# Scores and state products by head in 64x32 tiles, and a reordered first block, in a state-attention and two-FFN kernel

## The chip, the cores and the metric

The kernel runs on one core of a Trainium2 chip. A core has TensorE (PE in the profile; its weight loads are PEld), VectorE (DVE), ScalarE (ACT), GpSimd (POOL) and SyncE (SP), which here issues nearly all DMAs. SBUF is the working memory, PSUM holds eight banks of 128 partitions by 512 fp32 numbers into which TensorE writes. The metric is device time in microseconds (us), the median of three runs.

## The reference

```python
def _attn_ref(x, state):                     # x: 8 batches, 8 heads, 512 tokens, 64; state: 32 states
    scale = 1.0 / np.sqrt(D)
    scores = scale * np.matmul(x, state.transpose(0, 1, 3, 2))
    a = softmax(scores)                      # over the 32 states
    xread = np.matmul(a, state)
    scores2 = scale * np.matmul(state, x.transpose(0, 1, 3, 2))
    a2 = softmax(scores2)                    # over the 512 tokens
    sread = np.matmul(a2, x)
    return np.concatenate([xread, sread], axis=2)

x = attn_out as (8 * 544, 512)               # heads side by side
h = x @ w_in;  g = np.maximum(0.01 * h, h);  x = g @ w_out        # 512 -> 2048 -> 512
g = x @ w_gate;  out = (silu(g) * (x @ w_val)) @ w_out2           # 512 -> 1536 -> 512
```

The weights arrive as 64-bit floats; the kernel makes fp32 of them itself.

## The kernel before

**Layer 1 folds the reading of the states into w_in.** For tokens, `x_read @ w_in` equals `a @ (state @ w_in)`. So the kernel computes, for each batch b, each group g of 512 columns of w_in (four groups) and each head, a product of the 32 states with the 64 rows of w_in that belong to the head. Four heads make one half q (two pairs of heads p = 2q and 2q+1; a pair lies on 128 partitions, its two heads e on 64 each), so a tile `sw` of 128 rows (4 heads x 32 states) by 512 columns stands for (b, g, q). It is split into a high and a low part (`swh`, `swl`), and the attention `a` into `ah` and `al`; every product of large matrices is done as three passes (`passes`, L437): low times high, high times low, high times high.

**The products come in two ways.** Batch 0's are made in place: `state_win` (L452) multiplies `states`, a tile in which a pair's two heads stand block-diagonally (128 rows by 64 columns, zeros elsewhere, filled by ScalarE copies from the loaded tile `flat` in `place_states`), with a chunk of w_in; two such matmuls fill one PSUM bank, `keep_sw_h` (ScalarE) and `keep_sw_l` (VectorE) split it from the bank. All the others go through DRAM: `product_sw` (L461) multiplies, for one g and one pair, the states of four batches (bs = 0 or 1) of one head, 64 rows by 128 columns, with the head's half of the chunk; both heads go into two banks, ScalarE copies these to staging tiles, and `store_sw` writes them to `sw_dram` (for bs = 0 without batch 0's rows). There are 4 x 4 x 2 = 32 such products. Later `load_sw` fetches the 128 rows of one (b, g, q), and `split_sw_h` and `split_sw_l` split them.

**Scores.** `read_state` (L309) makes, for one b and q, the scores of 512 tokens: two matmuls of `states` (128 x 64) with the transposed tokens `xt` into one bank, a copy out (`scores_out`), the softmax over states on VectorE and ScalarE, and the split into `ah` and `al`. `read_tokens` (L374) makes the other softmax later: `turn` (four transposes, bank a), `read` (32-column products, bank b) and `read_out`.

**Slots.** Layer 1 runs in 8 x 16 slots, one for each batch j and each 128 of the 2048 hidden columns f. A slot has `h_mm` (six matmuls for the slot after next), `h_act` (leaky ReLU on ScalarE, high part on ScalarE, low part on VectorE) and `y_mm` (twelve matmuls into the four banks of `ps_y`). Other work is put into slots by `put` (L1306): it gives each step a start slot, waits for the step before, and moves a step on while VectorE's load in a slot (its "cost") would exceed a budget. A step's part W (ScalarE) runs at the head of the slot, D (VectorE) next, A after the first part of `h_act`, P (TensorE) and L (ScalarE) at the end. `sw_steps` load and split the products of later batches, `keep_steps` make batch 0's for g = 1 to 3 in the slots of `KEEP`.

**Opening and first block.** Everything is issued in program order, each engine taking its own instructions in that order. Before slot 0 the letters of `START` give the order, in slots 0 to 15 those of `SLOT0`: `c` advances by one of four steps the conversion of a weight chunk of 64-bit floats (two ScalarE operations, four VectorE operations: `limit`, `sign`, `join`, `add`; for chunks of w_out also a split into high and low), `p` makes one product that is ready, `0` and `1` the next step of batch 0's scores and softmax for q = 0 and 1, `h` a kept product of g = 0, `l` its low part, `m` and `M` the first hidden blocks; `H`, `S`, `L` are h_mm and the rest of h_act, `Y` and `Z` y_mm's halves, `D` and `A` the parts of the steps. `ORDER` is the order of the 32 chunks of w_in (`i`) and w_out (`o`), `LOADS` that of the first loads. A chunk of w_in is also stored to `win_dram`, for the 256 tail tokens at the end of layer 1. From slot 16 on the weights of layer 2 are converted in the background (`fill`).

PSUM banks: two for `ps_h`, four for `ps_y`, and banks a and b of `ps_a` for all else. Layer 2 (from about 690 us) is not touched.

Of the kernel before, what the change touches and what calls it, by code (L numbers as in the profile page):

```python
# [25 lines left out]
def kernel(  # L26
# [65 lines left out]
    SLOT0 = [  # L92
        "DcHcpAccccSYLpcZccc",
        "DcHcAcccpSYLpccZccc",
        "DcHcpccAcSYLpZccp",
        "cDccHcApSccYLpcZcccc",
        "cDcHccApScYLcZpc",
        "cccDHpccAccScYLpccZ",
        "ccDcHAcpScccYcLpZc",
        "ccDccHcApSccYcLpcZ",  # L100
        "cDcHcpcASYLpcccZ",
        "ccDHcAScYcpLccZcp",
        "ccDcHcASYcpLccZcp",
        "cDHccApSccYLccZ",
        "pcDHccASccYLcpcZ",
        "cpcDcHAccSYLccpccZp",
        "DcpcHcccpAcSYLcpZ",
        "pDpcHccpAcSYLcZp",
    ]
    KEEP = (0, 1, 3, 5, 8, 7)  # L110
# [39 lines left out]
    states = first1.tile([P, NPAIR, B, 2 * NS], F32, name="states")  # L150
# [10 lines left out]
    sw_dram = [[dram.tile([H, P, 512], F32, name=f"sw_dram{bs}_{g}") for g in range(FB)] for bs in range(B // 4)]  # L161
# [12 lines left out]
    def next_xt(n):  # L174
        for _ in range(min(n, len(pairs_t))):
            b, p = pairs_t.pop(0)
            xt[b, p] = xin.tile([P, S], F32, tag="xt", name="xt")
            nc.sync.dma_start(out=xt[b, p], in_=x_t[b, p])
# [54 lines left out]
    def convert(keys, room, prepare, load_next, finish=None):  # L233
# [4 lines left out]
        while todo or before or (finish and done):  # L238
# [15 lines left out]
            if key:  # L254
                ops["low"]()
                ops["sign"]()
# [52 lines left out]
    def read_state(b, q, bank):  # L309

        pairs = (2 * q, 2 * q + 1)
        v = {}

        def scores():

            ps = v["ps"] = ps_a.tile([P, 512], F32, tag=bank, name="ps_s")
            for i, p in enumerate(pairs):
                nc.tensor.matmul(  # L318
                    ps[2 * NS * i:2 * NS * (i + 1)], lhsT=states[:, p, b, :], rhs=xt.pop((b, p)),
                    start=True, stop=True,  # L320
                )
            next_xt(2)

        def scores_out():
            v["s"] = S_[b, q] = at1.tile([P, S], F32, tag="s", name="s", bufs=4)
            nc.scalar.copy(v["s"], v["ps"])


        def softmax_max():
            v["st"] = at1.tile([P, S], F32, tag="st", name="st", bufs=2)  # L330
            v["m1"] = at1.tile([P, S // NS], F32, tag="m1", name="m1", bufs=2)
            nc.vector.transpose(out=v["st"], in_=v["s"])
# [30 lines left out]
        def split_a_l():  # L363
# [3 lines left out]
            {"P": [scores], "L": [scores_out]},  # L367
# [6 lines left out]
    def read_tokens(b, q):  # L374
# [32 lines left out]
        def read():  # L407
# [3 lines left out]
            for i in range(2):  # L411
                for c in range(NC):
                    for k in range(4):
                        n = c * P + NS * (2 * i + k // 2)
# [37 lines left out]
    def state_win(b, g, q, bank):  # L452
        ps = (ps_y if bank == "y" else ps_a).tile([P, 512], F32, tag=bank, name="ps_sw")
        for i in range(2):
            nc.tensor.matmul(  # L455
                ps[2 * NS * i:2 * NS * (i + 1)], lhsT=states[:, 2 * q + i, b, :], rhs=raw["in", g, 2 * q + i],
                start=True, stop=True,
            )
        return ps

    def product_sw(g, p, bs, banks):  # L461

        pool = ps_y if banks == "yy" else ps_a
        ps = [pool.tile([P, 512], F32, tag=tag, name="ps_sw") for tag in banks]
        for e in range(2):
            half = slice(D * e, D * (e + 1))
            nc.tensor.matmul(  # L467
                ps[e], lhsT=flat[half, p, 4 * bs:4 * bs + 4, :].rearrange("d b n -> d (b n)"),
# [7 lines left out]
        unstored.append((g, p, bs, staged))  # L476
# [3 lines left out]
    def store_sw():  # L480
        while unstored:
            g, p, bs, staged = unstored.pop(0)
            for e in range(2):

                r = slice(NS, P) if bs == 0 else slice(0, P)
                nc.sync.dma_start(out=sw_dram[bs][g][2 * p + e, r], in_=staged[e][r])
# [17 lines left out]
    def keep_sw_h(g, q, ps):  # L504
        sw_ps[g, q] = ps
        split_h(sw_tiles(0, g, q)[0], ps)

    def keep_sw_l(g, q):
        split_l(SW[0, g, q][1], sw_ps.pop((g, q)), SW[0, g, q][0])

    def load_sw(b, g, q):
        assert not any((g, p, b // 4) in products for p in (2 * q, 2 * q + 1))
        if any((g, p, b // 4) == one[:3] for one in unstored for p in (2 * q, 2 * q + 1)):
            store_sw()
        t = SW_raw[b, g, q] = xin.tile([P, 512], F32, tag="sw", name="sw")
        rows = slice(NS * (b % 4), NS * (b % 4 + 1))
        nc.sync.dma_start(
            out=t, in_=sw_dram[b // 4][g][4 * q:4 * q + 4, rows]
# [71 lines left out]
    def y_out(j):  # L590
# [4 lines left out]
        else:  # L595
            two = [xin.tile([P, 2, n], F32, tag="xt", name="yst") for _ in range(KD // 2)]
# [569 lines left out]
    with tc.manual_schedule():  # L1166
# [27 lines left out]
        def finish1_h(key):  # L1194
            while any((KD * g + p) // 2 + NF1 // 2 == key[1] for g, p, _ in products):
# [105 lines left out]
        before = {}  # L1301

# [3 lines left out]
        def put(start, steps, kind=None, behind=2):  # L1306
# [3 lines left out]
            for k, step in enumerate(steps):  # L1310
                slot = max([start] + [t + 1 for t in at[-1:] + before.get(kind, [])[k + behind:k + behind + 1]])
# [19 lines left out]
        def keep_steps(g, q):  # L1331
            def product():
                pump_until(("in", g, 2 * q + 1))
                keep_sw_h(g, q, state_win(0, g, q, "b"))

            return [{"P": [product]}, {"D": [lambda: keep_sw_l(g, q)], "cost": 0.6, "now": True}]
# [4 lines left out]
        for g in range(1, FB):  # L1341
            for q in range(2):
                put(KEEP[2 * g - 2 + q], keep_steps(g, q), "keep")
        made = {0: 0, 1: 0}

        for n in range(2, 2 * B):
            start = max((n // 2 - 1) * NF1 + EARLY + 6 * (n % 2), start_tokens(n - 4) + 1) if n > 3 else 6 * (n % 2)
            r = put(start, read_state(n // 2, n % 2, "a"), "state")
            made[n] = r[1] + 1
            assert r[-1] < n // 2 * NF1 - 2, (n, r)  # L1350
# [8 lines left out]
        products[:] = [(g, p, bs) for g in range(FB) for p in range(NPAIR) for bs in range(B // 4)]  # L1359

        def pump_products(n, banks="ab"):
            for _ in range(n):
                one = next((one for one in products if ("in", *one[:2]) in ready), None)
                if one:
                    products.remove(one)
                    product_sw(*one, banks)

        keep = [(0, 0), (0, 1)]
        low = list(keep)

        flat = cv.tile([P, NPAIR, B, NS], F32, name="flat")
        for action in LOADS:
# [4 lines left out]
            else:  # L1377
                nc.sync.dma_start(
                    out=flat.rearrange("p k b n -> p (k b n)"), in_=state_t.rearrange("e d k b n -> (e d) (k b n)")
                )  # L1380
        nc.gpsimd.memset(states, 0.0)
        make_identity(nc, ident)

        def place_states(some):
            for e in range(2):
# [256 lines left out]
```

## Time and profile before

| | us |
|---|---|
| median of three runs | 1434.46 (1433.67 to 1435.19) |
| the profiled execution | 1433.87 |
| its span, first to last instruction | 1432.0 |
| TensorE busy | 1411.4 |
| VectorE busy | 964.5 |
| ScalarE busy | 731.7 |

The first batch's slots run from 41.5 to 152.9 us, the later batches take 71.3 to 73.3 us each up to 585.3 us, the last one has the tail beside it, and layer 2 begins near 690 us. Busy shares are averages over these stages; what ends a wait has to be read in each stage. PE is shown busy while matmuls are in flight, so a busy PE is not one at its peak.

### The profile page before, as it was taken

How to read it: one execution, taken by the hardware profiler on the slowest of the kernel's cores; microseconds unless marked ns; L12 is line 12 of the kernel's file. 1: busy time of each engine (PE TensorE's matmuls, PEld its weight loads, DVE VectorE, ACT ScalarE, POOL GpSimd, SP SyncE). 2: the span in 40 equal slices, each digit the busy share in tenths (PEclk: the TensorE clock that was granted, in tenths of full speed). 3: DMA queues.
4: the chain of work that ended last, by engine and by line, in shares of the span. 5: the costliest groups of instructions: out<-in, count | busy, mean ns of one | idle time of the engine just before them, and what ended most of it. 6: DMA issues, size and time to landing. Idle time of an engine off the chain costs nothing.

```text
span 1432.0 us, 21111 instructions
## 1 busy us (share of the span) xinstructions
PE 1411.4 (99%) x7422; PEld 1127.1 (79%) x7422; DVE 964.5 (67%) x1735; ACT 731.7 (51%) x1347; POOL 3.0 (0%) x8
## 2 busy tenths in 40 slices
PE   5999999999999999999999999999999999999998
PEld 1446777777777778888888888888888888988887
DVE  6887677677767777544365884659656697546675
ACT  6888656665666665644433543336333364333342
POOL 0000000000000000000000000000000000000000
PEclk9999999999999999999999999999999999999999
DMA  7896656667675646561566777677866778776664
GB/s 282 299 316 219 215 205 224 217 221 249 209 246 210 225 164 220 188 217 38 168 193 196 250 222 224 194 223 223 235 210 193 224 222 234 250 259 194 195 193 125
DMA packets 190042, 307.60 MB, mean 215 GB/s; under 512 B 48753, under 2 KB 75377, under 8 KB 188913
## 3 DMA queue, kind: packets, MB, share of 16 engines
q1 hardware_dynamic: 186640, 297.33, 64.9%
q10 hardware_dynamic: 3296, 8.91, 1.6%
q8 instruction: 60, 0.98, 0.3%
q14 instruction: 46, 0.37, 0.1%
HBM read 225.44 MB, written 80.74 MB: 214 GB/s over the span
## 4 chain that ended last, share of the span: by engine, by line
PE 96%; ACT 2%; DMA 1%; DVE 1%; issue 0%; SPq 0%; ACTq 0%
PE ps_y L443 24%; PE ps_x L766 18%; PE ps_o L976 16%; PE ps_h L443 14%; PE ps_s L766 9%; PE ps_a L766 5%; PE ps_t L443 2%; PE ps_sw L467 2%; PE ps_yt L443 2%; PE ps_o L443 1%; PE ps_s L318 1%; PE ps_r L415 1%; DMA ws<-in_dram 1%; PE ps_sw L455 1%; PE ps_a L401 0%; ACT sw L473 0%
## 5 line engine op out<-in xcount | busy, mean ns | idle before, releaser
L443 PE MATMUL ps_y<-gh,w_parts 128*128 128x512 f32 x1024 | 341.0, 392 | 0.1
L766 PE MATMUL ps_x<-yc,wq 128*128 128x512 f32 x1152 | 278.1, 389 | 0.0
L766 PEld LDWEIGHTS ps_x<-yc,wq 128*128 128x128 f32 x1152 | 216.2, 188 | 44.9
L443 PEld LDWEIGHTS ps_y<-gh,w_parts 128*128 128x128 f32 x1024 | 192.2, 188 | 56.5 <-issue 11.4
L976 PE MATMUL ps_o<-zh,wq 128*128 128x512 f32 (+1 forms) x696 | 209.4, 382 | 0.0
L443 PE MATMUL ps_y<-gl,w_parts 128*128 128x512 f32 x512 | 199.4, 389 | 0.0
L167 DVE TENSOR_TENSOR gl<-hs,gh 128x512 fp32r<-128x512 f32 (+1 forms) x144 | 95.0, 659 | 106.4 <-ACT gh L164 106.2
L559 ACT ACTIVATE hs<-ps_h 128x512 f32<-128x512 f32 (+1 forms) x144 | 82.6, 574 | 153.2 <-PE ps_h L443 151.7
L976 PEld LDWEIGHTS ps_o<-zh,wq 128*128 128x128 f32 x696 | 129.2, 188 | 25.3
L766 PE MATMUL ps_s<-yc,wq 128*128 128x512 f32 x576 | 146.1, 389 | 0.0
L976 PE MATMUL ps_o<-zl,wq 128*128 128x512 f32 (+1 forms) x348 | 132.8, 382 | 0.0
L766 PEld LDWEIGHTS ps_s<-yc,wq 128*128 128x128 f32 x576 | 108.1, 188 | 22.4
L795 ACT ACTIVATE sg<-C 128x512 f32<-128x512 f32 x72 | 45.5, 632 | 156.7 <-DVE C L791 156.7
L787 ACT COPY C<-ps_x 128x512 f32<-128x512 f32 x96 | 56.1, 584 | 124.5 <-PE ps_x L766 124.5
L443 PEld LDWEIGHTS ps_y<-gl,w_parts 128*128 128x128 f32 x512 | 96.1, 188 | 19.5
L443 PE MATMUL ps_h<-ah,swl 128*128 128x512 f32 x256 | 106.3, 415 | 1.1 <-DVE swl L167 1.1
L791 DVE TENSOR_TENSOR C<-ps_s,C 128x512 f32<-128x512 f32 x48 | 33.0, 688 | 108.0 <-PE ps_s L766 108.0
L443 PE MATMUL ps_h<-al,swh 128*128 128x512 f32 x256 | 100.1, 391 | 0.2 <-DVE al L167 0.2
L443 PE MATMUL ps_h<-ah,swh 128*128 128x512 f32 x256 | 100.2, 391 | 0.0
L164 ACT CAST gh<-hs 128x512 fp32r<-128x512 f32 (+1 forms) x144 | 85.7, 595 | 3.0
L796 DVE TENSOR_TENSOR sg<-C,sg 128x512 f32<-128x512 f32 x72 | 49.8, 692 | 48.0 <-ACT sg L795 48.0
L976 PEld LDWEIGHTS ps_o<-zl,wq 128*128 128x128 f32 x348 | 65.4, 188 | 12.6
(135 smaller groups left out, 2118.5 us busy)
## 6 DMA issues: line engine op xcount, KB each, us to landing
wq<-quad_gate SPq DMA_DIRECT2D x168, 256.0 KB
wq<-quad_val SPq DMA_DIRECT2D x168, 256.0 KB
wq<-quad_o SPq DMA_DIRECT2D x168, 256.0 KB
ws<-in_dram SPq DMA_DIRECT2D x68, 512.0 KB
sw<-sw_dram SPq DMA_DIRECT2D x56, 256.0 KB
quad_gate<-hl SPq DMA_DIRECT2D x24, 512.0 KB
quad_val<-hl SPq DMA_DIRECT2D x24, 512.0 KB
quad_o<-hl SPq DMA_DIRECT2D x24, 512.0 KB
```

The costliest lines, as they stand in the source:

```text
L164: nc.scalar.copy(dst, src)
L167: nc.vector.tensor_tensor(out=dst, in0=src, in1=hi.bitcast(F32), op=ALU.subtract)
L318: nc.tensor.matmul(ps[2 * NS * i:2 * NS * (i + 1)], lhsT=states[:, p, b, :], rhs=xt.pop((b, p)), start=True, stop=True,)
L443: nc.tensor.matmul(ps, lhsT=w, rhs=v, start=first and n == 0, stop=last and n == len(todo) - 1)
L467: nc.tensor.matmul(ps[e], lhsT=flat[half, p, 4 * bs:4 * bs + 4, :].rearrange("d b n -> d (b n)"), rhs=raw["in", g, p][half], start=True, s ...
L559: nc.scalar.activation(hs, ps[:, :n], AF.Prelu, alpha=0.01)
L766: nc.tensor.matmul(bank, lhsT=a, rhs=v, start=first and n == 0, stop=last and n == len(todo) - 1, skip_group_check=True,)
L787: nc.scalar.copy(t[0], src)
L791: nc.vector.tensor_tensor(out=kept[0], in0=bank, in1=kept[0], op=ALU.add)
L795: nc.scalar.activation(t[0], c, AF.Sigmoid)
L796: nc.vector.tensor_tensor(out=t[0], in0=c, in1=t[0], op=ALU.mult)
L976: nc.tensor.matmul(bank, lhsT=a, rhs=v, start=start and m == 0, stop=stop and m == 2, skip_group_check=True,)
```

## The change

- **By head.** A new function `by_heads` makes four matmuls of 64 x 32 (the states of one head) into the four 32-partition strips of a bank. The heads' row halves alternate from strip to strip, and in the other half q the other way round (`e = c % 2 ^ q`), so that the eight matmuls of two banks use eight different 64x32 tiles of the array. `scores(b, qs, banks)` makes both halves' scores of a batch in one step with banks a and b, `scores_out` copies both out; in the opening each half is made alone. The order of heads inside half 1 is swapped in pairs, which `read` and `store_sw` follow. The tile `states`, its memset and `place_states` are gone; `flat` is loaded in two DMAs, batch 0 first.
- **Batches 1 to 3.** They no longer go through `sw_dram`. `load_win` fetches a group's four chunks of w_in from `win_dram` (4 x 256 KB), `state_win` makes both banks with eight matmuls, and `keep_sw_h` and `keep_sw_l` split straight from the banks in the next slot. `product_sw` is left for batches 4 to 7: 16 instead of 32 products.
- **The planner.** A step with a P part now takes a slot for itself among P steps (`taken`). The scores of a batch are one step; batch 1's start at slot 8.
- **Order.** `LOADS`, `ORDER`, `START`, `SLOT0` and `KEEP` are new; `START` has no product. The conversion's `sign` comes one chunk later, with `limit`. The pools for `xt` and `sw` have four buffers instead of three.

```diff
-    LOADS = "xswxxwww"
-    ORDER = "iiiioiiooiioiioioiioioioiooooooo"
-    START = "spc0Scpccc0p0cpccpcc1ccchcc1cccpc1clcpp0hcccpclp1c01cpcmcc"
+    LOADS = "xsxwxwxwwwS"
+    ORDER = "iiiioiioioioiioooiiioiiooioooooo"
+    START = "pc0cccccccc0Pcc0cc1cc1cc0c1cchclc1cclcccmccmMMcmM"
     SLOT0 = [
-        "DcHcpAccccSYLpcZccc",
-        "DcHcAcccpSYLpccZccc",
...
+        "cDcccpHAccScLYcpccZc",
+        "ccDcHcAcccSYccLcZc",
...
-    KEEP = (0, 1, 3, 5, 8, 7)
+    KEEP = (1, 5, 9)
+    WIN0 = 5
+    FIRST = 8
...
             if key:
                 ops["low"]()
-                ops["sign"]()
+            if prev:
+                prev["sign"]()
...
+    def by_heads(b, q, ps, moving):
+        for c in range(4):
+            p, e = 2 * q + c // 2, c % 2 ^ q
+            half = slice(D * e, D * e + D)
+            nc.tensor.matmul(
+                ps[NS * c:NS * (c + 1)], lhsT=flat[half, p, b, :], rhs=moving[p][half], start=True, stop=True,
+            )
+
+    def scores(b, qs, banks):
+        tokens = {p: xt.pop((b, p)) for q in qs for p in (2 * q, 2 * q + 1)}
+        S_ps = {q: ps_a.tile([P, 512], F32, tag=bank, name="ps_s") for q, bank in zip(qs, banks)}
+        for q in qs:
+            by_heads(b, q, S_ps[q], tokens)
...
+    def state_win(b, g, moving, banks):
         pool = ps_y if banks == "yy" else ps_a
+        for q, tag in enumerate(banks):
+            sw_ps[b, g, q] = pool.tile([P, 512], F32, tag=tag, name="ps_sw")
+        for q in range(2):
+            by_heads(b, q, sw_ps[b, g, q], moving)
...
+    def load_win():
+        if wins:
+            _, g = wins.pop(0)
+            for p in range(NPAIR):
+                win[p] = xin.tile([P, 512], F32, tag="sw", name="win", bufs=4)
+                nc.sync.dma_start(out=win[p], in_=win_dram[g][:, p, :])
+
+    def state_win_loaded(b, g):
+        state_win(b, g, win, "ab")
+        load_win()
...
-                lhsT=flat[half, p, 4 * bs:4 * bs + 4, :].rearrange("d b n -> d (b n)"),
+                lhsT=flat[half, p, 4:8, :].rearrange("d b n -> d (b n)"),
...
+                while alone and slot in taken:
+                    slot += 1
+                if alone:
+                    taken.add(slot)
...
+        for g in range(1, FB):
+            put(KEEP[g - 1], [{"P": [lambda g=g: product0(g)]}, both(0, g)])
+        slots.setdefault(WIN0, []).append({"A": [load_win]})
         for b in range(1, B):
             for g in range(FB):
-                put(b * NF1 + 4 * g - 10, sw_steps(b, g))
+                if b < 4:
+                    put(b * NF1 + 4 * g - 7, [{"P": [lambda b=b, g=g: state_win_loaded(b, g)]}, both(b, g)])
+                else:
+                    put(b * NF1 + 4 * g - 10, sw_steps(b, g))
```

## Rows read from the trace of the kernel before

**Rows 1.** The page, part 1: each engine's busy time, share, instructions.
```profile
PE 1411.4 (99%) x7422; PEld 1127.1 (79%) x7422; DVE 964.5 (67%) x1735; ACT 731.7 (51%) x1347; POOL 3.0 (0%) x8
```

**Rows 2.** The page, part 4: shares of the chain of waits by engine.
```profile
PE 96%; ACT 2%; DMA 1%; DVE 1%; issue 0%; SPq 0%; ACTq 0%
```

**Rows 3.** Stretches (from:to, length, busy of each engine, granted clock, DMA share, GB/s).
```profile
core 0: us, PE busy (x) PEld busy (x) DVE busy (x) ACT busy (x) POOL busy (x), PEclk, DMA share, GB/s
19.00:26.00 7.00, 5.52 (x14) 1.46 (x12) 6.93 (x14) 4.93 (x11) 0.00 (x0) 1.00 0.87 312
26.00:33.00 7.00, 6.38 (x11) 1.97 (x12) 6.76 (x15) 4.76 (x10) 0.00 (x0) 0.51 1.02 313
33.00:41.50 8.50, 8.24 (x30) 4.30 (x28) 6.57 (x13) 8.46 (x17) 0.00 (x0) 1.00 0.92 325
41.50:136.50 95.00, 93.43 (x346) 48.42 (x345) 80.77 (x154) 80.23 (x150) 0.00 (x0) 1.00 0.86 294
136.50:152.90 16.40, 16.40 (x74) 13.38 (x72) 5.84 (x10) 7.01 (x13) 0.00 (x0) 1.00 0.52 143
226.20:298.10 71.90, 71.90 (x501) 57.16 (x500) 53.29 (x111) 44.21 (x81) 0.00 (x0) 1.00 0.69 236
```

**Rows 4.** Groups of TensorE instructions, 41.5 to 136.5 us (line, tiles, shapes, count | busy, mean ns).
```profile
L467 PE MATMUL ps_sw<-w_in,flat 64*128 64x512 f32 x98 | 29.4, 640 | 0.1
L455 PE MATMUL ps_sw<-w_in,states 128*64 128x512 f32 x24 | 8.0, 618 | 0.4 <-ACT sw L473 0.4
L318 PE MATMUL ps_s<-xt,states 128*64 128x512 f32 x8 | 2.1, 605 | 0.0
```

**Rows 5.** The same groups, 0 to 36 us.
```profile
L467 PE MATMUL ps_sw<-w_in,flat 64*128 64x512 f32 x28 | 12.5, 817 | 7.1 <-DVE w_in L224 5.4 <-ACT sw L473 0.9 <-DVE swl L167 0.8
```

**Rows 6.** Timeline of TensorE around one product (start us, length us, what).
```profile
40.14 0.39 PE L443 MATMUL ps_h<-ah,swh 128*128 128x512 f32 x1
40.46 1.13 PE L467 MATMUL ps_sw<-w_in,flat 64*128 64x512 f32 x4
41.52 0.50 PE L443 MATMUL ps_y<-gh,w_parts 128*128 128x512 f32 x1
41.85 0.39 PE L443 MATMUL ps_y<-gl,w_parts 128*128 128x512 f32 x1
```

**Rows 7.** Timeline of TensorE ahead of and behind one score pair.
```profile
159.56 0.39 PE L443 MATMUL ps_y<-gh,w_parts 128*128 128x512 f32 x1
...
161.22 0.39 PE L443 MATMUL ps_h<-al,swh 128*128 128x512 f32 x1
```

**Rows 8.** Chain of waits in order of time, two slots without extra work.
```profile
136.68 2.72 PE ps_y L443 x12
...
140.76 2.72 PE ps_y L443 x12
```

**Rows 9.** Timeline of VectorE in the opening: instructions after idle time [in brackets].
```profile
7.74 0.43 DVE L215 TENSOR_SCALAR w_in<-ws 128x512 int32<-128x512 int32 x1 [7.74 <-ACT ws L213]
...
9.95 0.71 DVE L332 STREAM_TRANSPOSE st<-s 128x512 f32<-128x512 f32 x1 [1.32 <-ACT s L326]
...
12.94 0.43 DVE L215 TENSOR_SCALAR w_in<-ws 128x512 int32<-128x512 int32 x1 [0.83 <-ACT ws L213]
...
18.52 0.43 DVE L215 TENSOR_SCALAR w_in<-ws 128x512 int32<-128x512 int32 x1 [3.50 <-ACT ws L213]
...
36.31 0.69 DVE L167 TENSOR_TENSOR al<-a,ah 128x512 fp32r<-128x512 f32 x1 [0.81 <-ACT ah L164]
```

**Rows 10.** Timeline of ScalarE in the opening.
```profile
5.12 1.28 ACT L1387 ACT_TABLE_LOAD   x1 [5.12 <-DMA flat<-in_dram]
...
16.85 1.07 ACT L473 COPY sw<-ps_sw 128x512 f32<-128x512 f32 x2 [2.84 <-PE ps_sw L467]
```

**Rows 11.** Timeline of TensorE in the first batch: a wait inside hidden matmuls.
```profile
57.88 0.50 PE L443 MATMUL ps_h<-ah,swl 128*128 128x512 f32 x1 [0.52 <-DVE swl L167]
```

**Rows 12.** Timeline of TensorE: products of four column strips into one bank.
```profile
169.75 0.76 PE L415 MATMUL ps_r<-xn,et 128*32 128x32 f32 x64
```

**Rows 13.** Timeline of TensorE in the opening: a kept pair.
```profile
28.62 1.97 PE L455 MATMUL ps_sw<-w_in,states 128*64 128x512 f32 x4
```

More of the change, by code (lines that the diff above doesn't have):

```diff
@@ L307, with scores_out, read_state @@
     A, S_ = {}, {}
-    def read_state(b, q, bank):
-        pairs = (2 * q, 2 * q + 1)
-        v = {}
[L314 to L326, printed above, removed]
+    def by_heads(b, q, ps, moving):
[10 more added lines that the diff above has]
+            by_heads(b, q, S_ps[q], tokens)
+        for q in qs:
+            S_[b, q] = S_ps[q]
+    def scores_out(b, qs):
+        for q in qs:
+            ps, S_[b, q] = S_[b, q], at1.tile([P, S], F32, tag="s", name="s", bufs=5)
+            nc.scalar.copy(S_[b, q], ps)
+        next_xt(2 * len(qs))
+    def read_state(b, q):
+        v = {}
         def softmax_max():
@@ L1194, in finish1_h @@
         def finish1_h(key):
-            while any((KD * g + p) // 2 + NF1 // 2 == key[1] for g, p, _ in products):
+            while any((KD * g + p) // 2 + NF1 // 2 == key[1] for g, p in products):
                 pump_products(1)
@@ L1301 @@
         before = {}
+        taken = set()
         def budget(slot):
@@ L1329, in sw_steps, with both @@
             ]
[L1331 to L1336, printed above, removed]
+        def both(b, g):
+            return {
+                "W": [lambda: keep_sw_h(b, g, 0), lambda: keep_sw_h(b, g, 1)],
+                "D": [lambda: keep_sw_l(b, g, 0), lambda: keep_sw_l(b, g, 1)],
+                "cost": 1.2,
+                "now": True,
+            }
@@ new lines @@
+        made = {0: 0, 1: 0}
+        for b in range(1, B):
+            start = max((b - 1) * NF1 + EARLY, start_tokens(2 * b - 4) + 1) if b > 1 else FIRST
+            step = {"P": [lambda b=b: scores(b, (0, 1), "ab")], "L": [lambda b=b: scores_out(b, (0, 1))]}
+            at, = put(start, [step], "scores")
+            for q in range(2):
+                steps = read_state(b, q)
+                if b == 1:
+                    steps = [step | {"now": True} for step in steps]
+                r = put(at + 1 + (6 * q if b > 1 else q), steps, "state", 2 if b > 1 else 4)
+                made[2 * b + q] = r[0] + 1
+                assert r[-1] < b * NF1 - 2, (b, q, r)
@@ L1357, in run, with pump_products @@
                     op()
-        products[:] = [(g, p, bs) for g in range(FB) for p in range(NPAIR) for bs in range(B // 4)]
-        def pump_products(n, banks="ab"):
+        products[:] = [(g, p) for g in range(FB) for p in range(NPAIR)]
+        def pump_products(n):
             for _ in range(n):
-                one = next((one for one in products if ("in", *one[:2]) in ready), None)
+                one = next((one for one in products if ("in", *one) in ready), None)
                 if one:
                     products.remove(one)
[L1366 to L1371, printed above, removed]
+                    product_sw(*one)
         for action in LOADS:
@@ L1416 @@
                 pump(1)
-        for step in list(halves[0]) + list(halves[1]):
-            for part in "DAPL":
-                run([step], part)
-        for g, q in keep:
-            pump_until(("in", g, 2 * q + 1))
-            keep_sw_h(g, q, state_win(0, g, q, "y"))
-        for g, q in low:
-            keep_sw_l(g, q)
+        assert not any([list(half) for half in halves] + [low])
         for f in range(2):
```

133 lines of the change are left out of this document (59 added, 74 removed).

## The prediction

> **What bounds the kernel now.** I read the engine line first: TensorE is busy for 1411.4 of 1432.0 us and no other engine passes 67% [rows 1]; and 96% of the chain of waits is TensorE [rows 2]. So a microsecond of TensorE work that goes comes off the end, unless its stage has another limit close behind. The table of stretches shows where that is so [rows 3]. From 226.2 to 298.1 us (the third batch) VectorE is busy for 53.3 of 71.9 us: only TensorE counts there. In slots 0 to 11 of the first batch (41.5 to 136.5 us) it is 93.4 us of TensorE, 80.8 of VectorE, 80.2 of ScalarE and 0.86 of the DMA engines: four limits within 15%. Before 41.5 us TensorE mostly waits.
>
> The prices come next. A slot with nothing extra lasts 4.08 us, from one batch of output products to the next [rows 8], 0.227 us a matmul over 18. A product of states and w_in stands between the 40.14 and the 41.85 us matmul; two ordinary ones would take 0.45 of those 1.71 us, so it **costs 1.26 us** [rows 6]. The same way, a pair of 128x64 score matmuls costs 161.22 - 159.56 - 0.45 = 1.21 us [rows 7]. I call each such group of fp32 matmuls a block.
>
> **Blocks, counted.** Before: 28 records of the product line lie ahead of 36 us, at four records a product 7 products [rows 5]; 24 follow in slots 0 to 11 (98 records, two of them the end of the product before) with 6 kept pairs and 2 score pairs [rows 4], one product lies between, and the plan puts the other 12 score pairs into slots 17 to 97. After, by the plan's arithmetic: 16 products, 3 kept groups of eight, 7 score groups of eight and 12 groups of eight for batches 1 to 3. In slots 0 to 11 that is 16 products and 5 groups (three kept, the scores of batch 1, and batch 1's first group); slot 13 has one more; from slot 16 on stand 10 + 6 = 16 groups for the former 12 score pairs: **four blocks more, 4 x 1.21 = +4.8 us**, all in stretches where only TensorE counts.
>
> **What a group of eight costs.** No row shows 64x32 tiles. Two row halves run side by side into two banks (four records, 1.13 us, [rows 6]); four column strips run side by side into one bank (64 small records in 0.76 us, [rows 12]), 0.012 us a record. The least is therefore a block as now, 1.06 us to the next matmul; sixteen records instead of four add at most 12 x 0.012 = 0.14 us. I take +0.05, since a strip is loaded while others stream. Over the 16 groups from slot 16 on **this is +0.8 us**, at most 2.2; in slots 0 to 11 VectorE hides it (below). The other end, no overlap of the halves, is a rival below.
>
> The rule that speaks against this change is in the Trainium skill, "TensorEngine Tiling (Array Packing)", Gotcha 1: row tiles write to different PSUM banks and cannot use one bank at the same time. Here each bank takes heads from both row halves. "PSUM — Partial Sum Buffer" (PSUM bank collisions) narrows it to a bank and 32 partitions, and the change gives no two halves the same of these at once. No row here shows either.
>
> **The opening, up to 41.5 us.** VectorE paces it. From its first instruction at 7.74 us to the last half of the attention's low part at 36.31 it idles 1.32 us (scores), 3.50 us (a ScalarE conversion that stands behind the copies of a product, which in turn waited 2.84 us for TensorE) and 0.81 us, and one more gap of 0.83 [rows 9, 10]. Without products and without the copies into the block-diagonal states, ScalarE is free (and SP, in whose queue the products' stores stand ahead of w_in loads, has fewer waits): the 3.50 and the 0.83 go, -4.3 us. Against this, both parts of batch 0's product now come only after the fourth w_in chunk, in one group, and VectorE waits for it: 1.97 us for such a group at the slow clock [rows 13], some 0.6 us for the ScalarE copy (two took 1.07 in [rows 10]), less 0.4 us of conversion that fits: +2.2 us. The first scores need a smaller load, but ScalarE's table load of 1.28 us, which now starts at 5.12 [rows 10], then sits behind them: I put this at nothing, between -1 and +1. So -2.1 us.
>
> TensorE then has less to do in the opening, and its clock matters: the granted share is 0.51 from 26 to 33 us, the 1.2 GHz level, after a stretch in which TensorE was busy for 5.52 of 7 us, and 1.00 from 33 on [rows 3]. With the products gone, the 18 matmuls of the first hidden blocks and one product may meet the slow level: 18 x 0.22 + 1 = 5 us of TensorE time, most of it while VectorE is still making the first operands. I take +0.6, between 0 and +4. The Trainium skill, "TensorE: Matmul & The Clock Gate", Part 1, says the slow clock is the default and activity lifts it; by that the upper end is the likelier, and the opening would gain nothing. The fall after a half-idle stretch agrees with it. **Opening: -1.5 us, between -4 and +2.**
>
> **Slots 0 to 11.** Before, TensorE's sum is 12 x 4.08 + 24 x 1.26 + 8 x 1.21 = 88.9 us, and the stretch took 95.0: 6.1 us of waits. They sit around the kept pairs: a hidden product waits 0.52 us for a kept product's low part, with the pipe drained before and after [rows 11]. After, TensorE's sum is 48.96 + 16 x 1.26 + 5 x 1.25 = 75.4 us. VectorE doesn't fall with it: the conversion steps in these slots go from 103 to 99 (one chunk less: two operations of 0.43 and two of 0.69 us as in [rows 9], -2.2), two low parts of batch 1's product come in earlier (+1.4), one low part of the attention slips out (-0.7), so 80.8 - 1.5 = 79.3 us. DMA: 0.86 x 95.0 = 82 us of engine time for 28 MB (294 GB/s); 32 stores of 256 KB stand where 50 of 256 and 192 KB stood, two loads of 1 MB come, five of 256 KB go, about 7% less, 76 us. So **VectorE becomes the bound of this stretch**, with TensorE and DMA some 4 us behind it. Floor 79.3. Kept groups fall from six to three and batch 1's first group works like one of them, so I add two thirds of today's waits, 4.1: 83.4 us, **-11.6 us**. The upper end is 93: VectorE, unlike TensorE today, waits for ScalarE and for landings as well, and twice the waits and more would then come.
>
> **Slots 12 to 15.** 16.4 us now [rows 3], all TensorE. One group for batch 1 (+1.25); slot 12 still has the second half of batch 1's softmax and conversions on VectorE, on which the next output products wait: +0.75, between 0 and 2.5. Together **+2.0 us**.
>
> **What hides the rest.** The loads of w_in for batches 1 to 3 (four of 256 KB instead of two) have three slots or more, 12 us, and the DMA engines stand at 0.69 there [rows 3]; uncovered, a late one would cost TensorE its lateness, up to 3 us a time. SP issues them behind a wait for the group before, and what is queued behind are loads with a slot's slack. ScalarE now waits at the head of a slot for that slot's product: its two copies (1.1 us) end while the hidden product (1.36 us) still runs, so its next operation is not late. Scores now take banks a and b at once; the transposes and reads that also use them stand in other slots. These I cost at nothing.
>
> **Sum.** -1.5 - 11.6 + 2.0 + 4.8 + 0.8 = -5.5 us. The profiled execution took 1433.87 us, 1.87 outside its span, and the median of three is 1434.46. So 1428.4 against the profiled one, 0.6 more, **1429 us**, against the median.
>
> **Rivals.** (1) *The halves don't overlap.* If two row halves can't write one bank together, a group of eight takes two streams: +0.9 us (a block's 1.06 less the drain). 22 groups from slot 0 on: +20, some 3 of it hidden: 1446 us, slower than before. It decides from 5.5 / 22 = +0.25 us a group, where the sum is zero. For it: no row shows two row halves writing one bank; against it: each kind of overlap by itself is in the rows [rows 6, 12]. The rule of the Trainium skill's "TensorEngine Tiling (Array Packing)", read by bank, would have it so. Then the change would not do what it says. (2) *The first block stays as long.* Four limits at over 90% wait on one another: slots 0 to 11 at 90 to 93 us, which is 6.6 to 9.6 us over the forecast: 1436 to 1438; with less of it 1434. For it: 6.1 us of waits already with TensorE alone near its limit. (3) *TensorE stays the bound.* The reorder lets VectorE run ahead out of a shorter opening; slots 0 to 11 at 79 us and the opening at -4: 1422 us. For it: the 80.8 us of VectorE were spread over 95 and its work is the same; against it: a first block without a wait.
>
> **Chances.** Forecast 0.52 (own range 1425 to 1432), halves 0.10, first block as long 0.22, TensorE-bound 0.16. The range takes in the last two, but not the halves: 1419 to 1438. A measurement tells about 0.2%, 2.9 us, from no change. Faster, below 1431.6: nearly nine tenths of the forecast and all of (3), 0.62; between 1431.6 and 1437.3: the rest of the forecast and most of (2), 0.22; slower: (1) and the end of (2), 0.16.
>
> **What would show it.** The opening: no gap of 3.5 us on VectorE ahead of 19 us, a new one of about 2 us ahead of the first low part, and the first output matmul near 40 us. Slots 0 to 11: about 83 us, VectorE over 90% busy, and output matmuls that wait for conversions. A group of eight: the next hidden product 1.0 to 1.2 us after its start; 1.9 would be rival (1). From slot 16 on: the third batch, 71.9 us now [rows 3], gets five groups for two score pairs and lasts 75 to 76, with no TensorE waits for w_in loads. I am wrong if those loads come late, if the first block keeps its 111 us, or if the first matmuls run at half clock into slot 1.

## The result and the profile after

| | before | after |
|---|---|---|
| median, us | 1434.46 (1433.67 to 1435.19) | 1421.40 (1420.77 to 1422.31) |
| the profiled execution, us | 1433.87 | 1422.31 |
| its span, us | 1432.0 | 1420.5 |

The ratio is 0.9909, with a 95% interval from 0.9895 to 0.9924: 13.1 us less, where 5.5 were forecast. The prediction had 1429, with 1419 to 1438 around it; 1421.4 lies in that range, which takes in two of its rivals, and below the forecast's own 1425 to 1432. The profiled execution of after is the slowest of its five, so the two spans lie only 11.5 us apart. Where these went, by stage of the profiled executions (a stage ends where the first output matmul of the next one starts):

| stage | before | after | difference | forecast |
|---|---|---|---|---|
| opening, up to slot 0 | 41.5 | 34.7 | -6.8 | -1.5 (-4 to +2) |
| slots 0 to 11 | 95.0 | 84.1 | -10.9 | -11.6 |
| slots 12 to 15 | 16.4 | 17.6 | +1.2 | +2.0 |
| slots 16 to 111 | 432.4 | 437.3 | +4.9 | +5.6 |
| the rest | 846.7 | 846.8 | +0.1 | 0 |

Three stages came out within 0.8 us of their terms. The opening did not: it gave 5.3 us more than forecast, and its own bounds did not hold it.

The page of after, parts 1 and 4, beside [rows 1, 2]: TensorE is busy for 14.8 us less, VectorE for 4.2 us more, and the chain of waits now has 3% of VectorE where it had 1%.

```profile
PE 1396.6 (98%) x7646; PEld 1121.4 (79%) x7646; DVE 968.7 (68%) x1735; ACT 712.8 (50%) x1311; POOL 1.2 (0%) x7
PE 94%; DVE 3%; DMA 1%; ACT 1%; issue 1%; SPq 0%; DVEq 0%; ACTq 0%
```

The stretches of after, with the columns of [rows 3]:

```profile
7.00:20.00 13.00, 5.89 (x18) 0.65 (x16) 11.45 (x22) 7.08 (x12) 0.00 (x0) 0.84 1.03 381
20.00:27.00 7.00, 2.79 (x8) 0.37 (x8) 6.83 (x15) 2.86 (x5) 0.00 (x0) 0.50 0.49 173
27.00:34.70 7.70, 7.36 (x26) 3.98 (x23) 7.37 (x15) 6.58 (x13) 0.00 (x0) 0.84 0.78 196
34.70:118.80 84.10, 79.86 (x357) 46.47 (x356) 77.58 (x144) 69.54 (x131) 0.00 (x0) 0.98 0.89 304
118.80:136.40 17.60, 17.60 (x89) 13.62 (x88) 11.36 (x21) 8.64 (x16) 0.00 (x0) 1.00 0.44 132
213.50:289.30 75.80, 75.80 (x574) 57.47 (x573) 53.37 (x112) 44.39 (x82) 0.00 (x0) 1.00 0.71 243
```

In slots 0 to 11 (34.70 to 118.80) VectorE is busy for 77.58 of 84.10 us, 92%; before it was 85%. The chain of waits, followed back from the end of this stretch, has 33.0 us of VectorE and 30.6 of TensorE in after; in before it has 69.4 us of TensorE and 0.7 of VectorE. The third batch (213.50 to 289.30) lasts 75.8 us, all of it TensorE.

The groups of TensorE instructions in slots 0 to 11, as in [rows 4]: 15 products of states and w_in (L487; the sixteenth stands just ahead of the stretch) and five groups of eight (L318). The last column says what TensorE waited for ahead of them: the products' copies out of the bank, a low part, a w_in conversion.

```profile
L487 PE MATMUL ps_sw<-w_in,flat 64*128 64x512 f32 x60 | 19.9, 669 | 2.3 <-ACT sw L493 1.7 <-DVE swl L169 0.4
...
L318 PE MATMUL ps_sw<-w_in,flat 64*32 64x512 f32 x48 | 4.3, 601 | 1.7 <-DVE w_in L226 1.7
L318 PE MATMUL ps_s<-xt,flat 64*32 64x512 f32 x16 | 1.1, 601 | 0.0
L318 PE MATMUL ps_sw<-win,flat 64*32 64x512 f32 x16 | 1.1, 601 | 0.0
```

Two groups of eight in the timeline of TensorE, first the scores of batch 1, then batch 1's product in slot 13. Start, length, what; the next matmul starts 1.02 us after the group's start in both.

```profile
94.03 1.09 PE L318 MATMUL ps_s<-xt,flat 64*32 64x512 f32 x16
95.05 0.50 PE L452 MATMUL ps_h<-ah,swl 128*128 128x512 f32 x1
...
125.71 1.09 PE L318 MATMUL ps_sw<-win,flat 64*32 64x512 f32 x16
126.73 0.50 PE L452 MATMUL ps_h<-ah,swl 128*128 128x512 f32 x1
```

A pair of 128x64 score matmuls of before, in the same view, has 1.01 us to the next matmul:

```profile
159.88 1.08 PE L318 MATMUL ps_s<-xt,states 128*64 128x512 f32 x4
160.89 0.50 PE L443 MATMUL ps_h<-ah,swl 128*128 128x512 f32 x1
```

The opening of after on TensorE, from the first part of batch 0's product to the first output matmul:

```profile
11.91 1.05 PE L318 MATMUL ps_sw<-w_in,flat 64*32 64x512 f32 x4 [0.36 <-DVE w_in L226]
17.05 1.92 PE L318 MATMUL ps_sw<-w_in,flat 64*32 64x512 f32 x4 [4.09 <-DVE w_in L226]
20.99 1.92 PE L318 MATMUL ps_sw<-w_in,flat 64*32 64x512 f32 x4 [2.02 <-DVE w_in L226]
26.13 1.92 PE L318 MATMUL ps_sw<-w_in,flat 64*32 64x512 f32 x4 [3.22 <-DVE w_in L226]
27.97 0.79 PE L452 MATMUL ps_h<-ah,swl 128*128 128x512 f32 x1
...
29.93 0.50 PE L452 MATMUL ps_h<-ah,swl 128*128 128x512 f32 x1 [0.34 <-DVE swl L169]
...
34.71 0.40 PE L452 MATMUL ps_y<-gh,w_parts 128*128 128x512 f32 x1
```

The group of eight is not run in one piece: its four parts (two heads each, two records for each matmul) start as their chunks of w_in are converted, at 11.91, 17.05, 20.99 and 26.13 us. The same stretch on VectorE, and ScalarE's table load:

```profile
8.07 0.71 DVE L342 STREAM_TRANSPOSE st<-s 128x512 f32<-128x512 f32 x1 [8.07 <-ACT s L333]
...
26.32 0.68 DVE L169 TENSOR_TENSOR swl<-ps_sw,swh 128x512 fp32r<-128x512 f32 x1
26.93 0.41 DVE L217 TENSOR_SCALAR raw<-ws 128x512 int32<-128x512 int32 x1
27.26 0.68 DVE L169 TENSOR_TENSOR al<-a,ah 128x512 fp32r<-128x512 f32 x1
...
29.19 0.68 DVE L169 TENSOR_TENSOR swl<-ps_sw,swh 128x512 fp32r<-128x512 f32 x1
```

```profile
0.73 1.28 ACT L333 ACT_TABLE_LOAD   x1 [0.73 <-PEq L1651]
```

No instruction of VectorE from 8.07 up to the last low part at 29.19 carries an idle time in brackets. Busy time of VectorE from its first instruction to the end of the last operand of the hidden blocks, first in after, then in before (length, busy, granted clock, DMA share, GB/s):

```profile
8.07:29.87 21.80, 21.11 (x41) 0.69 0.85 298
```

```profile
7.74:37.00 29.26, 22.29 (x44) 0.88 0.81 288
```

The stretch is 7.5 us shorter, 1.2 of it VectorE's work (three instructions fewer), 6.3 its idle time.

### The profile page after: what moved, and what is told of

It is laid out like the page before. It is cut to its first block, busy times and chain, and to the rows that moved or that the text cites. A ratio compares the mean times of both kernels' runs of the same rounds, so it can differ in the third digit from the quotient of the medians.

```text
span 1420.5 us, 21417 instructions
## 1 busy us (share of the span) xinstructions
PE 1396.6 (98%) x7646; PEld 1121.4 (79%) x7646; DVE 968.7 (68%) x1735; ACT 712.8 (50%) x1311; POOL 1.2 (0%) x7
## 4 chain that ended last, share of the span: by engine, by line
PE 94%; DVE 3%; DMA 1%; ACT 1%; issue 1%; SPq 0%; DVEq 0%; ACTq 0%
PE ps_y L452 23%; PE ps_x L783 18%; PE ps_o L993 16%; PE ps_h L452 14%; PE ps_s L783 9%; PE ps_a L783 5%; PE ps_t L452 2%; PE ps_yt L452 2%; PE ps_o L452 1%; PE ps_sw L318 1%; PE ps_r L424 1%; DMA ws<-in_dram 1%; PE ps_sw L487 1%; PE ps_s L318 1%; PE ps_a L410 0%
```

## The experiments

The theory going in: groups of eight cost no more than a pair because their eight tiles differ; slots 0 to 11 are VectorE's; the opening is short because VectorE no longer waits. Against it stood the prediction's rivals and two that the trace of after suggested: that a late load in slot 7, or the slow clock in the opening, sets what is left.

### Do the halves overlap because their tiles differ?

```diff
-            p, e = 2 * q + c // 2, c % 2 ^ q
+            p, e = 2 * q + c // 2, c % 2
...
-                        n = c * P + NS * (2 * i + (k // 2 ^ q))
+                        n = c * P + NS * (2 * i + (k // 2))
...
-                nc.sync.dma_start(out=sw_dram[g][2 * p + (e ^ p // 2)], in_=staged[e])
+                nc.sync.dma_start(out=sw_dram[g][2 * p + e], in_=staged[e])
```

> The changed kernel, but the heads' row halves alternate the same way in both banks, so that a group of eight uses four 64x32 tiles of the array twice instead of eight tiles once. Theory (the eight run side by side only because each has a tile of its own): a group that now takes 1.02 us to the next matmul takes about 1.9 us; from slot 16 on 16 groups, so the six batches there take 437.3 + 16 x 0.86 = 451 us, and the time is 1421.4 + 14 to 18 us, about 1437. Rival (the array takes the second half one stream later anyway, or the cost of a group is its issue): no change, within 1 us of 1421.4.

Measured: 1437.36 us, ratio 1.0022 (1.0013 to 1.0031), 16 us above after. A group in its timeline of TensorE:

```profile
101.93 1.92 PE L318 MATMUL ps_sw<-w_in,flat 64*32 64x512 f32 x16
103.78 0.50 PE L452 MATMUL ps_y<-gh,w_parts 128*128 128x512 f32 x1
```

With the row halves no longer swapped in half 1, the two banks' matmuls use the same four tiles, and the next matmul starts 1.85 us after the group's start instead of 1.02: +0.83 a group, where rival (1) had priced +0.9. Slots 16 to 111 take 450.7 us against 437.3, +13.4, which is 16 groups by 0.84. So the groups of eight cost no more than a pair only with the swap of the heads' order in half 1. Rival (1) had the right price, but not the right condition: each bank is written by heads of both row halves here as in after, and what differs is that four tiles are used twice.

### Is batch 0's product cheap because its parts run chunk by chunk?

The failed step had VectorE wait 2.2 us for a group that starts after the fourth chunk. Here it does: the part that needs the fourth chunk is issued first.

```diff
-    def by_heads(b, q, ps, moving):
+    def by_heads(b, q, ps, moving, order=(0, 1, 2, 3)):
...
-        for c in range(4):
+        for c in order:
...
-        for q in range(2):
-            by_heads(b, q, sw_ps[b, g, q], moving)
+        late = banks == "yy"
+        for q in (1, 0) if late else (0, 1):
+            by_heads(b, q, sw_ps[b, g, q], moving, (2, 3, 0, 1) if late else (0, 1, 2, 3))
```

> The changed kernel, but batch 0's first group of eight is issued with the pair of the fourth w_in chunk first, so that all eight matmuls wait for it, as the forecast had assumed. Theory (the group's matmuls run as each chunk is ready, and so the low parts cost VectorE no wait): VectorE waits 2 to 2.5 us ahead of the first low part, the first output matmul comes at 36.7 to 37.2 instead of 34.7 us, and some 2 us stand at the end, 1423.4. Rival (only the last two matmuls count, and the order of the eight is indifferent): no such wait, 34.7 us, 1421.4.

Measured: 1425.01 us (1423.22 to 1427.03), ratio 0.9942 (0.9927 to 0.9957), 3.3 to 4.7 us above after by the ratios (after has 0.9909, and 0.9919 when it was run again). TensorE, then VectorE:

```profile
26.35 1.96 PE L318 MATMUL ps_sw<-w_in,flat 64*32 64x512 f32 x16 [15.05 <-DVE w_in L226]
29.78 0.79 PE L452 MATMUL ps_h<-ah,swl 128*128 128x512 f32 x1 [1.47 <-DVE swl L169]
...
36.22 0.63 PE L452 MATMUL ps_h<-ah,swh 128*128 128x512 f32 x1
...
39.89 0.39 PE L452 MATMUL ps_y<-gh,w_parts 128*128 128x512 f32 x1
```

```profile
29.03 0.69 DVE L169 TENSOR_TENSOR swl<-ps_sw,swh 128x512 fp32r<-128x512 f32 x1 [2.40 <-ACT swh L166]
```

VectorE waits 2.40 us for the first low part: the failed step's figure, under the order that it assumed. The first output matmul comes at 39.9 us, 5.2 later than in after, though, and not 2 to 2.5. The last operand (the second low part) is complete at 32.58 us, 2.7 later than in after. The other 2.5 us are TensorE's clock: after 15 idle us it runs the hidden matmuls 0.43 us apart until 37.9 us, the 1.2 GHz level, where after's profile shows the higher level from 29.4 us. Some of the 5.2 us came back in slots 0 to 11, 80.7 us here.

### What did dropping the products from the opening do alone?

The kernel before, with the letters `p` taken out of `START` and nothing else changed; the products go to later slots.

```diff
-    START = "spc0Scpccc0p0cpccpcc1ccchcc1cccpc1clcpp0hcccpclp1c01cpcmcc"
+    START = "sc0Scccc00ccccc1ccchcc1cccc1clc0hccccl1c01ccmcc"
```

> The kernel before, without products in the opening: its seven are made in the first block instead. Theory (the products, through ScalarE's copies, held up VectorE's conversions): the first output matmul comes 4 to 5 us earlier than 41.5 us, and seven products at 1.26 us come into slots 0 to 15, so that the time is 1434.5 + 4 to 5, about 1439. Rival (the opening became shorter through the smaller first load and the missing copies into the block-diagonal states): 41 us and more, and about 1443.

Measured: 1446.51 us (1444.80 to 1447.18), ratio 1.0090 (1.0074 to 1.0105): slower than before by 13 us, more than either expectation. TensorE of its opening, and the stretch of its slots 0 to 11:

```profile
32.53 0.79 PE L443 MATMUL ps_h<-al,swh 128*128 128x512 f32 x1 [4.59 <-DVE al L167]
...
36.54 0.63 PE L443 MATMUL ps_h<-al,swh 128*128 128x512 f32 x1
...
39.94 0.50 PE L443 MATMUL ps_y<-gh,w_parts 128*128 128x512 f32 x1
```

```profile
39.90:149.20 109.30, 104.67 (x374) 52.51 (x373) 81.24 (x153) 87.92 (x163) 0.00 (x0) 1.00 0.83 278
```

The 3.50 us gap on VectorE goes, as the prediction said, and the last operand of the hidden blocks, the low part of the attention, is complete at 33.07 us (the line below) where it was at 37.00 [rows 9]: 3.9 us earlier, from the products alone.

```profile
31.79 1.28 DVE L167 TENSOR_TENSOR al<-a,ah 128x512 fp32r<-128x512 f32 x2
```

But the first output matmul is only 1.6 us earlier. Here the hidden matmuls run 0.43 us apart until 37.4 us, where in before products stood just ahead of them and the clock was up from 33 us on [rows 3]. Ten matmuls at 0.43 instead of 0.23 us are 2.0 of the 2.3 us that are lost again: the slow clock that the prediction feared. In after the last operand is complete at 29.87, and 4.8 us lie from there to the first output matmul, against 4.5 in before; it lost almost nothing. The products that were dropped have to be made later: slots 0 to 11 take 14.3 us more. Seven products at 1.26 us are 8.8 of it, and TensorE waits 3.1 us ahead of products, 3.0 of them for ScalarE's copies, where it waited 0.1 in before [rows 4]; the other 2.5 us were not followed up. Alone, taking the products out does not pay; in after half of them are gone.

### Is slot 7's long wait a loss of the change?

In after's profile slot 7 lasts 12.1 us. `load_win`'s 1 MB is issued by SP at 71.72 us, at the end of slot 5, ahead of weight chunks. Over slots 6 to 8 the DMA engines stand at 1.03; in slot 7 (78.96 to 91.09 us) ScalarE waits for a chunk and TensorE for ScalarE, and then 3.4 us pass at half clock. The lines of after, of SP, ScalarE, TensorE, and the stretch behind:

```profile
71.72 2.64 SPq L476 DMA_DIRECT2D win<-win_dram  x4
```

```profile
83.08 0.67 ACT L215 ACTIVATE ws<-ws 128x512 f32<-128x512 f32 x1 [2.23 <-DMA ws<-in_dram]
```

```profile
85.33 1.61 PE L487 MATMUL ps_sw<-w_in,flat 64*128 64x512 f32 x4 [1.71 <-ACT sw L493]
```

```profile
72.20:97.70 25.50, 23.79 (x105) 13.66 (x97) 21.82 (x41) 19.93 (x38) 0.00 (x0) 0.93 1.03 380
87.50:90.90 3.40, 3.40 (x9) 1.40 (x7) 2.81 (x6) 2.46 (x5) 0.00 (x0) 0.50 1.03 369
```

The test starts the load three slots earlier:

```diff
-    WIN0 = 5
+    WIN0 = 2
```

> The changed kernel, but the first load of w_in for batch 1 (1 MB) is issued at slot 2 instead of slot 5. Theory (slots 6 to 8 are held up by that load, which stands in front of the weight chunks while the DMA engines are at 1.0; slot 2 had 0.78): slot 7 falls from 12.1 us to 8 or 9, slots 0 to 11 from 84.1 to about 81.5, the time to about 1419. Rival (VectorE's own work bounds the stretch and the chunk would be late anyway, or the load only moves the hold-up to slots 3 and 4): 84 us, 1421.4.

Measured: 1420.39 us (1420.20 to 1421.05), ratio 0.9909 (0.9892 to 0.9925), which cannot be told from after. Slot 7 falls to 8.3 us and slots 0 to 11 to 80.6, but in this execution the clock rose only at 34.2 us and the first output matmul came at 36.5. To see which of this belongs to the kernel, after itself was run once more, beside the three runs that follow:

> The changed kernel once more, beside the others of this call. Theory (TensorE's clock rises in the opening at a moment that differs from execution to execution, and slot 7's 12.1 us is one execution's): the first output matmul comes between 34.5 and 37 us with the clock's rise between 29 and 35 us, slot 7 takes 8 to 12 us, and the time is 1420 to 1422. Rival (both are fixed by the kernel): 34.7 us, 12.1 us again.

Measured: 1421.49 us (1420.44 to 1423.44), ratio 0.9919 (0.9904 to 0.9933). Its profile has slot 7 at 9.8 us and ScalarE's wait for the chunk at 1.42 us, with no slow clock behind it. So 2.3 of the 12.1 us belonged to that one execution. The load costs slot 7 about 1.5 us: 9.8 against 8.3 here, and 9.8 against 8.3 again in the pair of runs with extra matmuls below. But the earlier load moves part of the wait: in its run slot 5 lasts 6.15 us against 5.14, with a wait of ScalarE for a chunk of 0.77 us. What is won cannot be told from nothing in the time of the kernel.

### Does VectorE bound slots 0 to 11?

The conversion's `limit` (one of its four operations on VectorE, 0.42 us each) is left out, in layer 1 and in the background of layer 2; the rest stands.

```diff
             if prev:
-                prev["limit"]()
+                pass
```

> The changed kernel without the conversion's limit operation (0.42 us of VectorE for each of the 68 chunks; it guards against numbers too large for fp32, of which these inputs have none). Theory (VectorE paces the opening and slots 0 to 11): the opening is 1.5 to 2 us shorter (six chunks at 0.34 us), slots 0 to 11 shorter by 4 to 8 us of the 26 x 0.34 = 8.8 that VectorE sheds, the time 1413 to 1416. Rival (the loads set slots 0 to 11, as the DMA engines are at 1.0 for half of them): the opening as in the theory, slots 0 to 11 within 2 us of before, 1418 to 1420.

Measured: 1416.41 us (1416.16 to 1417.88), ratio 0.9884 (0.9869 to 0.9898), 5.1 us below after in the same set; 2.6 us between the two profiled executions (the fastest of after run again, the slowest without `limit`), so half of the 5.1 us is in no profile. The opening is 0.4 us shorter (34.5 against 34.9 us), where both expectations had 1.5 to 2; VectorE's first instruction came 1.16 us later in this execution (9.35 against 8.19). Slots 0 to 11 of after run again, then without `limit`:

```profile
34.90:116.60 81.70, 78.25 (x357) 45.84 (x356) 77.39 (x144) 69.40 (x130) 0.00 (x0) 1.00 0.90 313
```

```profile
34.50:113.70 79.20, 77.73 (x358) 45.70 (x357) 68.94 (x121) 70.24 (x132) 0.00 (x0) 1.00 0.90 323
```

VectorE sheds 8.5 us and the stretch 2.5. VectorE did bound it, but only until TensorE, at 77.73 of 79.20 us, takes over. (TensorE's busy time holds matmuls in flight; by prices it has 75.4 us of work.) The chain of waits, followed back from the end of each stretch, shows the same:

| us of the chain | TensorE | VectorE | ScalarE | DMA |
|---|---|---|---|---|
| after run again | 34.4 | 28.9 | 10.3 | 5.1 |
| without `limit` | 54.5 | 5.8 | 13.7 | 5.2 |

The answer lies between the theory, which had 4 to 8 us, and the rival, which had at most 2. Whether the DMA engines, at 0.90, would be the next limit no run shows.

### Does the slow clock in the opening cost after anything?

Unused matmuls of 128 x 128 by 256 columns are put between the parts of batch 0's product, to keep TensorE busy; their results go nowhere. Alone, and with the earlier load:

```diff
+            if c % 2 and between:
+                for _ in range(between.pop(0)):
+                    nc.tensor.matmul(
+                        warm[0][:, :256], lhsT=flat[:, 0, 0:4, :].rearrange("d b n -> d (b n)"),
+                        rhs=flat[:, 1].rearrange("d b n -> d (b n)"), start=True, stop=True,
+                    )
...
+            between = [4, 2, 3]
```

> The changed kernel with nine matmuls whose result nobody reads (128x128 by 256 columns, fp32) between the four pairs of batch 0's first group, in TensorE's idle time of 13 to 26 us. Theory (the slow clock after TensorE's idle time costs the opening a part of what VectorE gained): the granted clock is at the upper level by 27 us, the eighteen hidden matmuls run 0.23 us apart, the first output matmul comes at 34 to 34.5 us, and the time falls by 0.5 to 1.5 us against the changed kernel beside it. Rival (VectorE's low parts set the first output matmul whatever the clock): no change, within 0.3 us; if the nine matmuls stand in front of a product that is ready, up to 1 us slower.

> Both: the nine matmuls in the opening and batch 1's first load of w_in at slot 2. Theory (the two waits are different ones and add): 1.5 to 3 us below the changed kernel beside it, 1418.5 to 1420. Rival (what one gives, the other's stretch takes back, since VectorE and the loads bound it): as the changed kernel, 1421.

Measured: 1420.21 us (1419.92 to 1422.72), ratio 0.9912 (0.9897 to 0.9927), and with the earlier load 1420.53 (1419.38 to 1421.73), ratio 0.9911 (0.9895 to 0.9928): neither can be told from after's 1421.49. The opening of the first of the two, as a stretch and on TensorE:

```profile
18.70:34.80 16.10, 11.44 (x45) 5.79 (x45) 15.76 (x32) 10.03 (x18) 0.00 (x0) 1.00 0.65 190
```

```profile
29.98 0.51 PE L458 MATMUL ps_h<-ah,swl 128*128 128x512 f32 x1 [1.86 <-DVE swl L169]
...
34.80 0.40 PE L458 MATMUL ps_y<-gh,w_parts 128*128 128x512 f32 x1
```

The clock is at its upper level from 18.7 us on, the first three hidden matmuls are done sooner, and TensorE then waits 1.86 us for the second low part: the first output matmul comes at 34.8, where after had it at 34.7. So in these runs, where the clock rose by 30 us, VectorE's second low part sets when the rest of the opening can run, and a faster TensorE ahead of it moves nothing. In the run with the earlier load the clock fell again from 27.7 to 34.5 us, and the first output matmul came at 36.9. Over the profiles of after's variants and of the experiment on before the two go together: a rise at 18.7, 29.4 or 30.0 us gives 34.5 to 34.9, a rise at 34.2 or 34.5 gives 36.5 and 36.9, at 37.4 or 37.9 gives 39.9. (One more, the kernel with the same four tiles, has 30.8 and 36.3; its VectorE began 1.5 us later than after's.) What makes the clock rise early in one execution and late in another was not settled. No variant that does the whole work can be told from after on the faster side.

## Why the prediction was right or wrong, step by step

**What bounds what: right.** TensorE alone counts from slot 16 on, and slots 0 to 11 passed from TensorE to VectorE, 92% busy in after and in the chain of waits with 33.0 us, where before had 0.7.

**Blocks and a group of eight: right.** The counts came out (the groups view shows 5 groups of 16 records in slots 0 to 11, slot 13 one more). A group stands for 1.02 us in the timeline, and slot 13 lasts 5.32 us against 4.08 without it: 1.24 us, where the forecast had 1.25 to 1.26. The extra +0.8 us for the sixteen records was too much: 16 groups by 1.24 less 12 pairs by 1.21 [rows 7] is +5.3, the slots gained 4.9. The third batch lasts 75.8 us, forecast 75 to 76, with no wait for the loads of w_in. The rule of the Trainium skill that spoke against it ("TensorEngine Tiling (Array Packing)", Gotcha 1) does not decide here: in after heads of both row halves write one bank, in strips of their own, and the group still takes 1.02 us, a pair's 1.01; what costs 0.83 us is the same tile twice, as the first experiment shows. The runs agree with the narrower rule, by bank and 32 partitions, of the Trainium skill's "PSUM — Partial Sum Buffer" (PSUM bank collisions), which quotes the broader one beside it.

**Slots 0 to 11: right, with VectorE's work put 1.8 us too high.** Forecast 83.4 us: 79.3 of VectorE and 4.1 of waits. After's two profiled executions show 84.1 and 81.7: 77.58 and 77.39 of VectorE, and 6.5 and 4.3 of waits; in the first of them the two errors nearly cancel. The forecast that output matmuls would wait for conversions is only a small part of it (0.3 us on `w_parts`, from the page); TensorE waits ahead of the products of states and w_in and of the kept groups, 2.3 and 1.7 us. The gap to the second limit, "some 4 us", was smaller: leaving out `limit` gave 2.5 us before TensorE took over.

**Slots 12 to 15: right in kind.** +1.2: the group's 1.24, and nothing of the 0.75 us that slot 12 was to lose; it lasts 4.1 us as before.

**The opening: the term that was mis-sized**, -6.8 us instead of -1.5. By its parts:

- The gaps of 3.50 and 0.83 us went, as forecast. The experiment on before alone shows the cause of the first: without products it is gone, while 1.32 and 0.84 stay and one of 0.27 us comes.
- The gaps of 1.32 and 0.81 us went too, which the sum had not. The 0.81 belongs to the products as well: it is gone in the same experiment (both low parts of the attention stand in one line, 31.79), and in before two copies of a product (34.67 to 35.76) stand on ScalarE ahead of the high part that VectorE waits for. For the 1.32 us the new order is the reading, not shown by a run of its own: it gives VectorE the first scores as its first instruction (8.07) instead of a conversion and then a wait. No run separates it from the smaller first load and the copies into the block-diagonal states that are gone. The table load that the prediction set at nothing moved to 0.73 us, ahead of everything: its earlier place, 5.12 [rows 10], came from a wait on `flat` of the copies that the change removed.
- **The step that failed is "+2.2 us, VectorE waits for batch 0's product".** It took the group of eight for one block that starts when its last operand is there. TensorE takes its instructions in order, but each waits only for its own chunk: three of the four parts were done by 22.9 us, the first half's low part needed only the first two, and the second half's low part (29.19) came behind work that filled the time. With the group's order reversed VectorE waits 2.40 us, so the price was right, and the dependence was wrong. The two signs that the prediction named for it did not come in after: no gap ahead of the first low part, and the first output matmul at 34.7 us, not near 40.
- VectorE has 1.2 us less work ahead of the last operand (44 instructions then, 41 now), which the prediction did not count, and starts 0.33 us later.
- The clock: +0.6 forecast. From the last operand to the first output matmul it is 4.8 us, before 4.5: +0.3. The two runs with the earlier load have 6.9 us here, with the clock up at 34.2 and 34.5, so they lose 2 us and the range of 0 to +4 was a fair one. Its upper end, which the prediction took as the likelier by the Trainium skill's "TensorE: Matmul & The Clock Gate" (Part 1), showed in neither profile of after. Two of its readings of before's TensorE were too strong: the stretch that it calls half idle (19 to 26 us) was 79% busy [rows 3], and before 41.5 us TensorE does not mostly wait, it is busy for 26.58 of 41.50 us.

Together: -6.28 of idle time, -1.18 of work, +0.33 of a later start, +0.32 at the end: -6.81 us, which is the opening's difference. Of the 5.3 us that the sum lacked, 2.2 are the wait that did not come, 2.1 the gaps of 1.32 and 0.81 us, and 1.2 VectorE's work; the later start takes 0.3 back.

**The rivals.** (1) had the right price, 0.83 us a group for its 0.9, but not the mechanism: two row halves do write one bank together, and it takes the same tile twice to bring the price about. With it the first experiment is slower than before, at 1437 us, not 1446, because after had more in hand than the sum said. (2) did not happen. (3), at 1422 us, has the measured time, but not for its reason: it took 4 us from slots 0 to 11 by a TensorE bound that is not there; the time came from the opening. That 1421.4 lies in the wide range is owed to this rival's being taken in, and so is partly luck.

## What to carry to other kernels

Read the dependence of a group of instructions on an in-order engine from each instruction's own operands, and cost a wait only for the last of them whose result somebody needs then. When many small matmuls are to run side by side, count the distinct tiles: here eight of 64 x 32 cost as one stream, the same four used twice as two. And when a stage has several engines at over 90%, relieving the one that bounds it may be worth only the distance to the next, here 2.5 of 8.5 us.

## What was unexpected of the hardware

Two row halves of TensorE write into one bank at the same time, in different strips of 32 partitions, at no loss: 16 records in 1.02 us to the next matmul, against 1.85 us when the two banks' tiles coincide. The granted clock rose to its upper level at 29.4 us in one execution and at 34.2 in another of kernels whose openings are the same instruction for instruction, and the first output matmul moved with it by 1.8 us (34.7 and 36.5). And a wait of TensorE of 1.71 us in slot 7 was followed 2.2 us later by 3.4 us at half clock in one profile of after; in the other the wait there was 0.92 us, and the clock stayed up.
